# Attention followed by a mixture of experts: the last features turned by TensorE, the second expert prepared earlier, the loop count read later, output scatters without order

## Chip, cores and metric

One NeuronCore of a Trainium2 chip runs the whole program in one launch. The metric is device time in microseconds, median of the runs shown; lower is better.

## The reference

Eight batches of eight heads, 576 positions and 64 features go through causal attention with a decay from cumulated forget gates. The 4608 result rows (512 features) are then sent through one of eight experts each.

```python
decay = cum[:, :, :, None] - cum[:, :, None, :]
attn = softmax(where(causal, -1e9, scale * q @ k.T + decay))
x = (attn @ v).transpose(0, 2, 1, 3).reshape(4608, 512)
e_idx = argmax(x @ w_gate, axis=1)
gate_w = softmax(x @ w_gate)[e_idx];  eom = sigmoid(x @ w_output_gate)
for e in range(8):
    mask = e_idx == e
    out[mask] = gate_w * eom[mask, e] * (relu(x[mask] @ w1[e]) @ w2[e])   # 512 -> 1024 -> 512
```

## The kernel before

**Attention** (`attention`, lines 772 to 910) is a hand-written software pipeline: a loop over steps in which each part of the work has an offset in `OFF`, and the order of issue within a step is the string `OFF["order"]`. All engines run under a manual schedule, so each works through its instructions in the order of the program text. The features of a batch come in two units u = 0 to 15 (two per batch, four heads each). `feats` splits a unit into a high and a low f16 part (`x16`; ACT casts, DVE subtracts), `feats_turn` (line 527) turns each of the unit's four or five row tiles with a DMA transpose issued by SP into `xT`, and `feats_out` (line 534) writes `x16` to the DRAM buffer `xbuf`, also by SP. Units 0 to 14 are turned in the pipeline; unit 15 is made and turned behind it (lines 1039 to 1043).

**Routing** (`route`, lines 555 to 656) is a generator with one small operation per step: router matmuls on `xT`, argmax, rank within the expert, and at last one indirect DMA per row tile (POOL, line 649) that scatters row number and weight into the list `tbl`. Seven batches are routed in the pipeline; the last one is routed beside the first expert.

**Experts.** Rows of an expert are fetched by `gather_ids` (list from `tbl`, SP), `gather_rows` (indirect DMA by POOL, line 708) and `gather_turn` (DMA transpose by SP, line 714). Weights arrive as f32 (`fetch_w1`, `fetch_w2`, by SP, in four buffers each) and are split into f16 and bf16 parts by ACT and a subtraction (`split_w1`, line 666, `split_w2`, line 926). `up_products` and `up_split` make the hidden layer in eight column tiles fc (three matmuls for each of four k; ACT takes the high part out of PSUM, line 995, DVE the low one, line 996); `down_sum` makes one output tile of 128 rows (24 matmuls) and `down_out` (line 1017) evicts it by ACT and scatters it into the output by an indirect DMA of POOL.

**The start of the experts** (lines 1038 to 1080) is what the change is about. Expert 0 begins before the last batch is routed, on its first 384 rows, listed, gathered and turned in the pipeline (`early_gather`). Its order before: unit 15 is made and turned, first four W1 pieces of expert 1 fetched, the eight fc of expert 0 with steps of the last route between them (`OFF["steps"]`: one at fc 5, eight at 6, one at 7), three scatters of `tbl`, four W1 splits on DVE, the first output tile, `late_ids` (row numbers of the last 256 rows worked out on PE without waiting for `tbl`), gather and turn of these rows, the rest of the scatters, lists of expert 1, output tiles 1 and 2, gathers of expert 1, W1 pieces 4 to 7, the `up` of the late rows, turns of expert 1, two late output tiles, and at last all of W2 of expert 1 (line 1080).

**The main loop** (lines 1110 to 1146) runs expert 1 (n = 0) and then the other six, with the next expert's rows and weights fetched one stage ahead. In n = 0, behind the second output tile, `overflow_slots` (line 936) works out on DVE how many row tiles don't fit into the capacities, and reads that count into a register of every engine (line 972). The register is the bound of the loop of line 1148, behind everything.

Of the kernel before, what the change touches and what calls it, by code (L numbers as in the profile page):

```python
# [59 lines left out]
    "mv": ["xr", "v0", "v1"], "begin": -18, "wg": -4, "spread/1": -11,  # L60
    "before_late": 3, "steps": [0, 0, 0, 0, 0, 1, 8, 1], "dve": [181, 183, 185, 187, 189, 191],
    "order": "reduce put feats1 v0 scores nrec max pair rows spread feats0 fetch "
# [12 lines left out]
def _attn_moe(ctx, tc, qk, vm, f, wg, w1, w2, out):  # L75
# [451 lines left out]
    def feats_turn(u, t):  # L527
        b, hh = divmod(u, 2)
        if t < NC + b % 2:
            xT, x16 = xTs[u]  # L530
            nc.sync.dma_start_transpose(xT[:, t].rearrange("p j k n -> p (j k) n"),
                                        x16[:, t].rearrange("p j n -> p (j n)"))

    def feats_out(u):
        b, hh = divmod(u, 2)
        x16 = xTs[u][1]
        xv = xbuf[:, hh * DM:(hh + 1) * DM]
        nc.sync.dma_start(xv[b * S:b * S + SM].rearrange("(c p) d -> p c d", p=P),
                          x16[:, 0:NC].rearrange("p c j d -> p c (j d)"))
        if b % 2:  # L540
            for bb in (b - 1, b):
                r0 = (bb % 2) * SR
                nc.sync.dma_start(xv[bb * S + SM:(bb + 1) * S], x16[r0:r0 + SR, NC].rearrange("p j d -> p (j d)"))
# [228 lines left out]
    def attention():  # L772
# [12 lines left out]
        for s in range(OFF["begin"], last + OFF["nrest"] + 1):  # L785
# [36 lines left out]
            def turns():  # L822

                for t in range(NTB):
                    v, r = divmod(s - OFF["fturn"] - OFF["fturnstep"] * t, 12)
                    if r == 0 and 0 <= v < NQ - 1:
                        feats_turn(v, t)
# [108 lines left out]
    def overflow_slots():  # L936

        with tc.tile_pool(name="ov", bufs=1) as ov:
# [32 lines left out]
            nc.vector.tensor_copy(ncum, fl(cum)[0:1, E * G - 1:E * G])  # L971
        return nc.values_load(ncum, min_val=0, max_val=(NT - min(CAPS)) // P + E)

# [42 lines left out]

    def down_out(x, y, t):
        ids = x[0]
        ys = m2.tile([P, DM], F32, name="ys", bufs=3)
        nc.scalar.activation(out=ys, in_=y, func=AF.Copy, scale=ids[:, t, 1:2].bitcast(F32))  # L1020
        nc.gpsimd.indirect_dma_start(  # L1021
            out=out, out_offset=bass.IndirectOffsetOnAxis(ap=ids[:, t, 0:1], axis=0),
            in_=ys, in_offset=None, bounds_check=NT - 1, oob_is_err=False)

    def down(w2s, x, h, t0, t1):
        for t in range(t0, t1):
            down_out(x, down_sum(w2s, h, t), t)

# [3 lines left out]
    def load_w1(we, fc, raws=None, eng=nc.gpsimd):  # L1032
        return split_w1(m2, raws[fc] if raws else fetch_w1(m2, we, fc, 4), 8, eng)
# [3 lines left out]

    with tc.manual_schedule(engines=ENGINES):
        for part in range(2):
            feats(NQ - 1, part)  # L1040
            for t in (range(2), range(2, NTB))[part]:
                feats_turn(NQ - 1, t)
        feats_out(NQ - 1)
        late_before()
        W1r = [fetch_w1(m2, w1[1], fc, 4) for fc in range(4)]
        chain = route(B - 1)
        first = [(0, EARLY)]
        h = hidden()
        for fc in range(NF):
            hp = up_products(W1, x, first, fc)  # L1050
            for _ in range(OFF["steps"][fc]):
                next(chain, None)
            up_split(hp, h, first, fc)
        begun = len(scatters)
        while len(scatters) < begun + OFF["before_late"]:
            next(chain)
        W1n = [load_w1(w1[1], fc, W1r, nc.vector) for fc in range(4)]
        y = down_sum(W2, h, 0)
        at = late_ids()
        for t in range(ET, CT):  # L1060
            gather_rows(x, t, NT, at[:, t - ET:t - ET + 1])
            gather_turn(x, t)
        for _ in chain:
            pass
        down_out(x, y, 0)
        x1 = gather_ids(m2, tbl[NT:NT + CAP], CT)
        xl = gather_ids(m1, tbl[EARLY:CAP], CT - ET, ET, (m1.tile([P, CT, 2], I32, name="idsl"), x[1]))
        down(W2, x, h, 1, ET)
        for t in range(2):
            gather_rows(x1, t)  # L1070
        W1r += [fetch_w1(m2, w1[1], fc, 4) for fc in range(4, NF)]
        up(W1, x, [(EARLY, CAP)], h)
        for t in range(2, CT):
            gather_rows(x1, t)
        for t in range(CT):
            gather_turn(x1, t)
        W1n += [load_w1(w1[1], fc, W1r, nc.vector) for fc in range(4, NF)]
        down(W2, xl, h, ET, CT)
        W1, x = W1n, x1
        W2 = weights(load_w2, w2[1])  # L1080

# [28 lines left out]
        for n in range(len(CAPS) + 1):  # L1110
# [22 lines left out]
            for t in range(tiles):  # L1133
# [8 lines left out]
                down_out(x, y, t)  # L1142
                if not n and t == 1:
                    nsl = overflow_slots()
            if nx:
                e, x, W1, W2 = nx, x1, W1n, W2n

    with tc.For_i(0, nsl, 1) as i:
# [5 lines left out]
        h = up(weights(load_w1, w1[bass.ds(ei, 1)].rearrange("a f p k n -> (a f) p k n")), x, [(0, P)])  # L1154
        down(weights(load_w2, w2[bass.ds(ei, 1)].rearrange("a f p n -> (a f) p n")), x, h, 0, 1)

# [44 lines left out]
```

## Time and profile before

| | us |
|---|---|
| median of 3 runs (lowest to highest) | 821.77 (820.77 to 822.31) |
| the profiled execution, its own time | 827.2 |
| its span, first to last instruction | 825.5 |
| PE busy in it | 750.3 (91%) |
| POOL busy | 469.8 (57%) |
| DVE, ACT busy | 338.7, 338.6 (41% each) |

PE runs the matmuls; PEld is its weight load, which overlaps. An engine's time is busy time of instructions; a wait is told as the idle time before an instruction, with the event that came last. SP appears by its queue of DMA issues. The granted clock is TensorE's, as a share of 2.4 GHz.

### The profile page before, as it was taken

The page shows a single profiled execution, that of the slowest core. Times are in us where ns is not written, and L with a number is a line of the kernel's source. Part 1 is how long each engine was busy: PE and PEld are TensorE (multiplying, and loading weights), DVE is VectorE, ACT ScalarE, POOL GpSimd, SP SyncE. Part 2 cuts the span into 40 slices and gives each one's busy share as a digit, 9 for nine tenths or more (in the row PEclk, how much of TensorE's full clock was granted, in tenths as well). Part 3 has the DMA queues.
Part 4 walks back from the last instruction along what each step waited for, and adds up shares of the span by engine and source line. Part 5 has one row for each costly group of instructions (what it writes and reads, how often), then busy time and mean ns, then how long its engine had stood idle before and what let it go on. Part 6 is the DMA issues. An engine that isn't in the chain of part 4 may idle for free. (4 is left out here: it accounts for less than half of the span.)

```text
span 825.5 us, 21338 instructions
## 1 busy us (share of the span) xinstructions
PE 750.3 (91%) x8704; PEld 459.3 (56%) x8704; DVE 338.7 (41%) x774; ACT 338.6 (41%) x758; POOL 469.8 (57%) x517
## 2 busy tenths in 40 slices
PE   1699999899999999977979795999999999999995
PEld 0377777667776777755536462554544445444442
DVE  4446576575868576745502422120311203021020
ACT  6055565455655464644303321242342424333230
POOL 8088778688888888875143523345353644635321
PEclk9999999999999999989989897999999999999999
DMA  3343757958595678437868545265472745727210
GB/s 101 123 131 79 169 160 165 162 132 166 132 196 137 134 147 154 90 79 122 136 123 202 158 71 136 74 175 168 153 212 68 201 151 158 204 84 220 84 50 37
DMA packets 131689, 112.34 MB, mean 136 GB/s; under 512 B 94792, under 2 KB 104194, under 8 KB 131588
## 3 DMA queue, kind: packets, MB, share of 16 engines
q1 hardware_dynamic: 120020, 74.92, 40.4%
q10 hardware_dynamic: 4176, 17.11, 7.8%
q0 software_dynamic: 7392, 18.92, 7.7%
q8 instruction: 69, 1.13, 0.6%
q14 instruction: 32, 0.26, 0.1%
HBM read 72.52 MB, written 20.21 MB: 112 GB/s over the span
## 5 line engine op out<-in xcount | busy, mean ns | idle before, releaser
L380 POOL TENSOR_TENSOR plo<-p 128x512 f16<-128x512 f32 x186 | 197.5, 1076 | 69.5 <-ACT p L378 65.5
L986 PE MATMUL hp<-xT,w1h 128*128 128x512 f16 (+2 forms) x960 | 180.5, 304 | 16.2 <-DMA xT<-xg 9.9
L996 DVE SCALAR_TENSOR_TENSOR hl<-hp,hh 128x512 f16<-128x512 f32 (+2 forms) x120 | 54.0, 484 | 297.3 <-ACT hh L995 278.8
L296 DVE TENSOR_REDUCE nR<-mx 128x2 f32<-128x1024 f32 (+4 forms) x160 | 126.5, 807 | 92.2 <-PE mx L270 79.9
L378 ACT ACTIVATE p<-sc 128x512 f32<-128x512 f32 x192 | 112.8, 594 | 77.5 <-PE sc L270 69.1
L270 PE MATMUL sc<-qk 64*128 64x512 f32 (+4 forms) x640 | 136.7, 488 | 0.0
L1012 PE MATMUL y<-w2h,hh 128*128 128x512 f16 x312 | 119.2, 382 | 9.2 <-DVE ncum L971 9.2
L1013 PE MATMUL y<-w2l,hh 128*128 128x512 bf16 x312 | 119.2, 382 | 0.0
L1014 PE MATMUL y<-w2h,hl 128*128 128x512 f16 x312 | 119.0, 381 | 0.0
L986 PEld LDWEIGHTS <-w1h 128*128 128x128 f16 x960 | 76.3, 99 | 75.3 <-issue 13.4
L986 PE MATMUL hp<-xT,w1l 128*128 128x512 f16 (+2 forms) x480 | 114.3, 304 | 0.0
L995 ACT ACTIVATE hh<-hp 128x512 f16<-128x512 f32 (+2 forms) x120 | 46.8, 433 | 140.6 <-PE hp L986 132.7
L1021 POOL DMA_INDIRECT out_dram<-ys,ids x37 | 36.8, 995 | 102.5 <-ACT ys L1020 65.7
L270 PEld LDWEIGHTS <-pick 64*128 64x128 bf16 (+1 forms) x1152 | 64.1, 99 | 47.5 <-issue 25.6
L1020 ACT ACTIVATE ys<-y,ids 128x512 f32<-128x512 f32 x37 | 25.4, 687 | 137.2 <-issue 77.7
L930 POOL TENSOR_TENSOR w2l<-w2r,w2h 128x512 bf16<-128x512 f32 x28 | 32.2, 1153 | 82.1 <-ACT w2h L929 82.1
L270 PE MATMUL mx<-qk 64*128 64x256 bf16 (+5 forms) x384 | 64.6, 313 | 14.6 <-DVE nR L296 9.1
L452 PE MATMUL av<-Vs,p 128*128 128x65 f16 x640 | 69.9, 194 | 8.1 <-ACT xr L499 4.7
L454 PE MATMUL av<-Vs,plo 128*128 128x65 f16 x640 | 69.2, 193 | 4.6 <-POOL plo L380 4.6
L453 PE MATMUL av<-Vs,p 128*128 128x64 bf16 x640 | 69.5, 196 | 0.0
L270 PE MATMUL mx<-Ek,Eq 63*128 63x256 f16 (+5 forms) x384 | 58.5, 308 | 11.5 <-DMA Ek<-d 11.4
L670 POOL TENSOR_TENSOR w1l<-w1r,w1h 128x512 bf16<-128x512 f32 x48 | 54.6, 1162 | 21.5 <-ACT w1h L669 21.1
(178 smaller groups left out, 1380.7 us busy)
## 6 DMA issues: line engine op xcount, KB each, us to landing
qk<-in_qk_dram ACTq DMA_DIRECT2D x29, 576.0 KB
w1r<-in_w_dram SPq DMA_DIRECT2D x64, 256.0 KB
w2r<-in_w_dram SPq DMA_DIRECT2D x64, 256.0 KB
v<-in_vm_dram SPq DMA_DIRECT2D x16, 576.0 KB
xbuf<-x SPq DMA_DIRECT2D x16, 512.0 KB
qk<-in_qk_dram SPq DMA_DIRECT2D x3, 576.0 KB
xT<-x SPq DMA_TRANSPOSE x72
Eq<-mts SPq DMA_DIRECT2D x64, 0.1 KB
```

The costliest lines, as they stand in the source:

```text
L270: nc.tensor.matmul(dst(i), w(i), x(i), start=start, stop=stop)
L296: nc.vector.tensor_reduce(o, x, axis=AX.X, op=ALU.max, negate=True)
L378: nc.scalar.activation(out=f32, in_=src, func=AF.Exp, scale=0.125)
L380: eng.tensor_tensor(lo, f32, upper(f32), op=ALU.subtract)
L452: nc.tensor.matmul(dst, ph, vv[:, 0:W], start=kc == 0, stop=False)
L453: nc.tensor.matmul(dst[:, 0:D], ph, vv[:, W:].bitcast(BF16), start=False, stop=False)
L454: nc.tensor.matmul(dst, pl, vv[:, 0:W], start=False, stop=kc == qc)
L670: (eng or nc.vector).tensor_tensor(l, raw, h, op=ALU.subtract)
L986: nc.tensor.matmul(m[:, 0:c1 - c0], w[:, k], x, start=k == 0 and i == 0, stop=k == ND - 1 and i == 2)
L1012: nc.tensor.matmul(y, hh[:, fc, sl], wh, start=fc == 0, stop=False)
L1013: nc.tensor.matmul(y, hh[:, fc, sl], wl, start=False, stop=False)
L1014: nc.tensor.matmul(y, hl[:, fc, sl], wh, start=False, stop=fc == NF - 1)
```

## The change

The DMA transposes of units 14 and 15 go. `feats_turn_here` turns a unit with 20 transposes on TensorE into PSUM (tiles of the expert stage, two named hp1 and one y) and five evictions (three by ACT, two by DVE): unit 14 ahead of everything in the expert stage, unit 15 behind fc 1. The steps of the last route move forward, and so do the late rows (at fc 6, ahead of all five scatters of `tbl`). All eight W1 and W2 pieces of expert 1 are fetched and split in three portions of `ahead`, each in front of an output tile of expert 0, all subtractions on DVE; expert 1's gathers and turns all stand ahead of the late `up`. `overflow_slots` moves behind output tile 3 of n = 0 and its register read to output tile 0 of n = 2. Output scatters outside the loop are declared independent of one another.

```diff
-    "before_late": 3, "steps": [0, 0, 0, 0, 0, 1, 8, 1], ...
+    "steps": [0, 0, 1, 8, 1, 4, 4, 0], "turned": 1, "late": 6, ...
+    def feats_turn_here(u):
+        xT, x16 = xTs[u]
+        ms = [pm.tile([P, 512], F32, name=n, bufs=2).bitcast(F16) for n in ("hp1", "hp1", "y")]
+        for t in range(NTB):
+            for j in range(4):
+                nc.tensor.transpose(ms[t // 2][:, (t % 2 * 4 + j) * P:(t % 2 * 4 + j + 1) * P],
+                                    x16[:, t].rearrange("p j n -> p (j n)")[:, j * P:(j + 1) * P], identh)
+        for t in range(NTB):
+            dst, src = xT[:, t].rearrange("p j k n -> p (j k n)"), ms[t // 2][:, t % 2 * 512:t % 2 * 512 + 512]
+            if t % 2:
+                nc.vector.tensor_copy(dst, src)
+            else:
+                nc.scalar.copy(out=dst, in_=src)
...
-                    if r == 0 and 0 <= v < NQ - 1:
+                    if r == 0 and 0 <= v < NQ - 2:
                         feats_turn(v, t)
...
-        return nc.values_load(ncum, min_val=0, max_val=(NT - min(CAPS)) // P + E)
+        return ncum
...
+        if not looped:
+            for other in written:
+                tc.declare_no_dep(ins.ins, other.ins, reason="distinct rows")
+            written.append(ins)
...
+        feats_turn_here(NQ - 2)
         for part in range(2):
             feats(NQ - 1, part)
-            for t in (range(2), range(2, NTB))[part]:
-                feats_turn(NQ - 1, t)
         feats_out(NQ - 1)
         late_before()
         W1r = [fetch_w1(m2, w1[1], fc, 4) for fc in range(4)]
+        W2r = [fetch_w2(w2[1], fc) for fc in range(4)]
...
             for _ in range(OFF["steps"][fc]):
                 next(chain, None)
+            if fc == OFF["late"]:
+                at = late_ids()
+                for t in range(ET, CT):
+                    gather_rows(x, t, NT, at[:, t - ET:t - ET + 1])
+                    gather_turn(x, t)
             up_split(hp, h, first, fc)
-        begun = len(scatters)
-        while len(scatters) < begun + OFF["before_late"]:
-            next(chain)
-        W1n = [load_w1(w1[1], fc, W1r, nc.vector) for fc in range(4)]
-        y = down_sum(W2, h, 0)
-        at = late_ids()
-        for t in range(ET, CT):
-            gather_rows(x, t, NT, at[:, t - ET:t - ET + 1])
-            gather_turn(x, t)
+            if fc == OFF["turned"]:
+                feats_turn_here(NQ - 1)
+        W1n, W2n = [], []
+        def ahead(fc):
+            W1n.append(load_w1(w1[1], fc, W1r, nc.vector))
+            if fc + 4 < NF:
+                W1r.append(fetch_w1(m2, w1[1], fc + 4, 4))
+            W2n.append(split_w2(W2r[fc], nc.vector))
+            if fc + 4 < NF:
+                W2r.append(fetch_w2(w2[1], fc + 4))
         for _ in chain:
             pass
-        down_out(x, y, 0)
+        for fc in range(3):
+            ahead(fc)
+        down_out(x, down_sum(W2, h, 0), 0)
         x1 = gather_ids(m2, tbl[NT:NT + CAP], CT)
         xl = gather_ids(m1, tbl[EARLY:CAP], CT - ET, ET, ...)
-        down(W2, x, h, 1, ET)
-        for t in range(2):
+        for fc in range(3, 6):
+            ahead(fc)
+        down_out(x, down_sum(W2, h, 1), 1)
+        for t in range(CT):
             gather_rows(x1, t)
-        W1r += [fetch_w1(m2, w1[1], fc, 4) for fc in range(4, NF)]
-        up(W1, x, [(EARLY, CAP)], h)
-        for t in range(2, CT):
-            gather_rows(x1, t)
+        for fc in range(6, NF):
+            ahead(fc)
+        down_out(x, down_sum(W2, h, 2), 2)
         for t in range(CT):
             gather_turn(x1, t)
-        W1n += [load_w1(w1[1], fc, W1r, nc.vector) for fc in range(4, NF)]
+        up(W1, x, [(EARLY, CAP)], h)
         down(W2, xl, h, ET, CT)
-        W1, x = W1n, x1
-        W2 = weights(load_w2, w2[1])
+        W1, W2, x = W1n, W2n, x1
...
-                if not n and t == 1:
-                    nsl = overflow_slots()
+                if n == 0 and t == 3:
+                    ncum = overflow_slots()
+                if n == 2 and t == 0:
+                    nsl = nc.values_load(ncum, min_val=0, max_val=(NT - min(CAPS)) // P + E)
```

## Rows read from the trace of the kernel before

**Rows 1.** Busy time by stretch (the view of windows): stretch from : to in us, its length, busy us and instruction count of PE, PEld, DVE, ACT and POOL, then the granted TensorE clock (1.00 is 2.4 GHz), the DMA share and GB/s. The first four are stretches right behind an idle time of PE, the last is the kernel's second half.

```profile
388.30:391.80 3.50, 3.49 (x12) 1.68 (x13) 0.00 (x0) 0.00 (x0) 2.28 (x3) 0.51 0.63 140
...
428.40:432.70 4.30, 4.30 (x21) 3.05 (x22) 0.42 (x1) 0.38 (x1) 0.87 (x1) 0.50 0.90 282
...
464.50:470.40 5.90, 5.86 (x23) 3.30 (x23) 1.11 (x3) 0.00 (x0) 2.07 (x2) 0.51 0.60 181
...
506.60:511.30 4.70, 4.66 (x12) 1.64 (x12) 0.00 (x0) 1.14 (x2) 2.26 (x2) 0.50 0.62 40
...
525.00:817.20 292.20, 292.20 (x1750) 141.86 (x1748) 53.55 (x112) 98.59 (x205) 126.53 (x121) 1.00 0.49 142
```

**Rows 2.** What PE waited for from 384 us to the end (the view of waits): the waiting instruction <- its releaser: total us, times, longest us.

```profile
PE hp L986 <- DMA xT<-xg: 9.9, 2, 5.7
PE y L1012 <- DVE ncum L971: 9.2, 1, 9.2
PE hp L986 <- DVE hl L996: 5.6, 1, 5.6
PE hp L986 <- issue: 0.7, 1, 0.7
```

**Rows 3.** The timeline of PE between 384 and 425 us: start, us, engine, line, operation, out<-in, count, and in brackets the idle time before it and what ended it.

```profile
383.88 0.18 PE L609 MATMUL rk<-runs,ones 128*128 128x32 bf16 x1
388.31 0.76 PE L986 MATMUL hp<-xT,w1h 128*128 128x384 f16 x2 [4.26 <-DMA xT<-xg]
...
422.31 0.38 PE L1014 MATMUL y<-w2h,hl 128*128 128x512 f16 x1
```

**Rows 4.** The timeline of SP's DMA queue from 380 to 450 us (issue times).

```profile
380.74 1.19 SPq L531 DMA_TRANSPOSE xT<-x  x1
382.02 2.63 SPq L714 DMA_TRANSPOSE xT<-xg  x2
...
392.42 8.67 SPq L531 DMA_TRANSPOSE xT<-x  x5
...
404.26 0.46 SPq L731 DMA_DIRECT2D had<-tbl  x1
404.76 1.92 SPq L663 DMA_DIRECT2D w1r<-in_w_dram  x4
423.56 2.68 SPq L714 DMA_TRANSPOSE xT<-xg  x2
426.51 0.39 SPq L702 DMA_DIRECT2D ids<-tbl  x1
```

**Rows 5.** The timeline of POOL from 356 to 384 us.

```profile
360.50 1.25 POOL L649 DMA_INDIRECT tbl<-rec,pi  x1 [0.17 <-issue]
...
371.77 1.34 POOL L708 DMA_INDIRECT xg<-xbuf,ids  x1 [0.15 <-issue]
```

**Rows 6.** The timeline of SP's DMA queue from 363 to 384 us.

```profile
366.00 0.40 SPq L702 DMA_DIRECT2D ids<-tbl  x1
...
375.57 1.23 SPq L714 DMA_TRANSPOSE xT<-xg  x1
```

**Rows 7.** The timeline of POOL from 408 to 424 us.

```profile
410.48 1.48 POOL L649 DMA_INDIRECT tbl<-rec,pi  x1 [1.79 <-DVE so L634]
...
414.05 0.96 POOL L649 DMA_INDIRECT tbl<-rec,pi  x1 [0.22 <-issue]
415.32 1.06 POOL L708 DMA_INDIRECT xg<-xbuf,lids  x1 [0.30 <-issue]
```

**Rows 8.** The timeline of PE from 424 to 530 us: two of the 128x256 matmul groups at full clock.

```profile
433.45 0.38 PE L986 MATMUL hp<-xT,w1h 128*128 128x256 f16 x2
433.67 0.27 PE L986 MATMUL hp<-xT,w1l 128*128 128x256 f16 x1
433.77 0.38 PE L986 MATMUL hp<-xT,w1h 128*128 128x256 f16 x2
```

**Rows 9.** The instructions of line 345 (the kernel's only transposes on TensorE), with duration min/median/max in ns.

```profile
L345 PE MATMUL mt<-identh,mh x32: 222/222/272, 26.5 to 357.4; 128*9 128x128 f16 x32
```

**Rows 10.** The timeline of ACT from 378 to 530 us: one eviction of each kind, with the idle time before it.

```profile
396.04 0.49 ACT L995 ACTIVATE hh<-hp 128x384 f16<-128x384 f32 x1 [1.46 <-PE hp L986]
...
422.73 0.69 ACT L1020 ACTIVATE ys<-y,ids 128x512 f32<-128x512 f32 x1 [4.49 <-PE y L1014]
...
435.94 0.38 ACT L995 ACTIVATE hh<-hp 128x256 f16<-128x256 f32 x1 [0.93 <-PE hp L986]
```

**Rows 11.** The timeline of DVE from 378 to 530 us.

```profile
387.19 0.42 DVE L147 TENSOR_TENSOR x<-xr,x 128x256 f16<-128x256 f32 x1
...
505.95 0.13 DVE L971 CAST ncum<-ov 1x1 int32<-1x1 f32 x1
```

**Rows 12.** Groups of ACT's instructions by line between 400 and 470 us: count, busy us, mean ns, idle before.

```profile
L669 ACT CAST w1h<-w1r 128x512 f16<-128x512 f32 x8 | 4.5, 619 | 0.3 <-DMA w1r<-in_w_dram 0.3
```

**Rows 13.** The same for DVE.

```profile
L670 DVE TENSOR_TENSOR w1l<-w1r,w1h 128x512 bf16<-128x512 f32 x8 | 5.0, 685 | 0.0
```

**Rows 14.** The instructions of line 972 (the loop count's read), duration min/median/max in ns.

```profile
L972 PEldq TENSOR_LOAD <-ncum x1: 487/487/487, 506.1 to 506.1; - x1
```

**Rows 15.** The timeline of POOL from 812 us to the end.

```profile
813.11 0.97 POOL L1021 DMA_INDIRECT out_dram<-ys,ids  x1 [4.21 <-ACT ys L1020]
819.76 0.98 POOL L1021 DMA_INDIRECT out_dram<-ys,ids  x1 [5.69 <-POOLq L1148]
```

More of the change, by code (lines that the diff above doesn't have):

```diff
@@ L60 @@
     "mv": ["xr", "v0", "v1"], "begin": -18, "wg": -4, "spread/1": -11,
-    "before_late": 3, "steps": [0, 0, 0, 0, 0, 1, 8, 1], "dve": [181, 183, 185, 187, 189, 191],
+    "steps": [0, 0, 1, 8, 1, 4, 4, 0], "turned": 1, "late": 6, "dve": [181, 183, 185, 187, 189, 191],
     "order": "reduce put feats1 v0 scores nrec max pair rows spread feats0 fetch "
@@ L1015, in down_sum, with down_out @@
         return y
-    def down_out(x, y, t):
+    written = []
+    def down_out(x, y, t, looped=False):
         ids = x[0]
@@ L1020, in down_out, with down @@
         nc.scalar.activation(out=ys, in_=y, func=AF.Copy, scale=ids[:, t, 1:2].bitcast(F32))
-        nc.gpsimd.indirect_dma_start(
+        ins = nc.gpsimd.indirect_dma_start(
             out=out, out_offset=bass.IndirectOffsetOnAxis(ap=ids[:, t, 0:1], axis=0),
             in_=ys, in_offset=None, bounds_check=NT - 1, oob_is_err=False)
-    def down(w2s, x, h, t0, t1):
+        if not looped:
+            for other in written:
+                tc.declare_no_dep(ins.ins, other.ins, reason="distinct rows")
+            written.append(ins)
+    def down(w2s, x, h, t0, t1, looped=False):
         for t in range(t0, t1):
-            down_out(x, down_sum(w2s, h, t), t)
+            down_out(x, down_sum(w2s, h, t), t, looped)
     def weights(load, we):
@@ L1154, in _attn_moe @@
         h = up(weights(load_w1, w1[bass.ds(ei, 1)].rearrange("a f p k n -> (a f) p k n")), x, [(0, P)])
-        down(weights(load_w2, w2[bass.ds(ei, 1)].rearrange("a f p n -> (a f) p n")), x, h, 0, 1)
+        down(weights(load_w2, w2[bass.ds(ei, 1)].rearrange("a f p n -> (a f) p n")), x, h, 0, 1, True)
 _INS = ['q', 'k', 'v', 'f', 'moe_w_gate', 'moe_w_output_gate', 'moe_w1', 'moe_w2']
```

## The prediction

> **What bounds the kernel now.** I read the page's slices of PE first: behind the start, those below 8 tenths all lie between 350 and 520 us. The view by stretch says it sharply: from 525 to 817 us PE works 292.20 of 292.20 us at full clock [rows 1], so nothing there can be won without taking matmuls away, which the change doesn't do. What can be won is PE's idle time in the start of the experts. The list of PE's waits behind 384 us has 9.9 us in two waits for turned rows, 9.2 for the loop count, 5.6 for DVE and 0.7 without a releaser [rows 2], 25.4 in all. The reader should then look at what follows each long wait: four stretches of 3.5, 4.3, 5.9 and 4.7 us at a granted clock of 0.50 or 0.51 [rows 1], the lower level of 1.2 GHz. The engine had stood still for 4.26, 5.7, 5.6 and 9.2 us before them; the 0.7 us one is followed by no such stretch. Half of these 18.4 us, 9.2, is lost too. So at most 25.4 + 9.2 = 34.6 us lie there.
>
> **The change part by part.** Each PE wait is taken in order, in the profiled execution's time.
>
> *First wait (turned rows of expert 0, 4.26 us).* PE ends attention at 383.88 + 0.18 = 384.06 and starts the up at 388.31 [rows 3]. SP issued the second and third early turns from 382.02 to 384.65, behind a unit 14 turn that started only at 380.74 [rows 4]; landing took 388.31 - 384.65 = 3.66. The first early turn started at 375.57 [rows 6], 2.46 behind the end of its gather (371.77 + 1.34) [rows 5]. Without the unit 14 turn the other two can be issued some 3.7 earlier, at 380.9, and land near 384.6. PE meanwhile does the 20 transposes of unit 14. No row shows such a block transpose in sequence. From below: three 128x256 matmuls follow one another in 433.77 - 433.45 = 0.32 [rows 8], 0.055 per 128 columns; from above: the one existing transpose lasts 0.222 alone [rows 9]. Back to back in independent PSUM columns they are nearest to the former: 20 x 0.055 = 1.1. The up starts at 385.2 instead of 388.31 (-3.1), and without a long idle time the half clock goes too (-1.75): -4.85.
>
> *Unit 15 on TensorE:* another 1.1 us on the path, +1.1. Its source was ready at 387.19 + 0.42 [rows 11]; unit 14's three ACT evictions of 0.6 (the mean of a 128x512 ACT cast is 0.619 [rows 12]) push it to about 389.2, and two fc of 1.95 each (eviction 0.49 and 1.46 idle before it [rows 10]) end on PE at 385.2 + 3.9 = 389.1. The cover is exact, so I add nothing but keep 1 us for the range. Ten SP turns of 1.2 to 1.7 us (five in 8.67) [rows 4] go; nothing on PE waited for them, but SP comes to its weight fetches at about 395 instead of 404.76 [rows 4]. There the read of the row list stands in front (it was at 404.26 [rows 4]) and must now wait for the scatters of batch 6; that wait is inside the 395.
>
> *Second wait (late rows, 5.66 us; half clock 2.15; and the 0.7).* Before, the late gathers started at 415.32, behind three scatters of the list [rows 7], and their turns at 423.56 [rows 4]. Now the row numbers are ready after fc 6, near 402.5, the two gathers end near 405, and with the 2.46 of rows 5 and 6 they land near 407.5, the turns near 412.5. PE ends the three early output tiles (5.18 each: 0.69 and 4.49 idle [rows 10]) at about 419.5, against 422.31 + 0.38 = 422.69 before [rows 3], so the late up finds its rows. All three go: -8.5.
>
> What is late next is the weights' last portion. The five scatters stand behind the gathers on POOL, cost 1.3 to 1.8 each with what lies between (410.48 to 414.05 held two, 414.05 to 415.32 one) [rows 7], and end near 412.5. Expert 1's list was read 366.00 - (360.50 + 1.25) = 4.25 behind the last scatter [rows 5, 6], so near 416.7 SP goes on, and only then fetches W1 and W2 piece 7, which stand behind this read on SP. Two 256 KB pieces land 2.5 to 4 us later. ACT does two casts of 0.62 [rows 12] on them, then the third output tile, and only then the first late hidden tile, which is due at 420.8; with two PSUM buffers PE runs on until 422.2. DVE's subtraction of 0.685 [rows 13] stands in the same way. With the fastest landing PE waits 0.9 us, with the slowest that I find without a further fault 3. I take 2.0: +2.0.
>
> *Third wait (DVE, 5.59 us, half clock 2.95).* It comes from the W2 splits of expert 1 standing ahead of its first hidden tiles on ACT and DVE; they are now done at 423. Expert 1's rows need lists, five gathers and five turns, about 435, while PE arrives near 442. -8.5.
>
> *Fourth wait (loop count, 9.20 us, half clock 2.35).* PE stood until the count was cast at 505.95 [rows 11]. Behind tile 3 of n = 0 the same DVE chain ends beside the first hidden tile of n = 1, and at n = 2 the count is long there. What stays is the read itself, 0.487 on PE [rows 14]: at least 0 if matmuls already issued cover it, at most its length. -11.55 + 0.5 = -11.05.
>
> *Output scatters* never gate PE. At the end the last scatter starts 819.76 - 813.11 = 6.65 behind the one before it [rows 15], 1.47 more than the tile time of 5.18. Without the wait for its predecessor that may shrink; between -1.5 and +0.5 I take 0, since the last eviction still has to come first.
>
> Sum: -4.85 + 1.1 - 8.5 + 2.0 - 8.5 - 11.05 = -29.8 us. The span would be 825.5 - 29.8 = 795.7. The profiled execution took 827.2, 5.4 over the median of 821.77; I take the difference over to the median: **792.0 us**.
>
> **Rivals.** *A. The late rows come later and the front stays short of weights.* For it: the one late gather in the trace ended at 415.32 + 1.06 = 416.38 and its turn started 7.2 us later [rows 4, 7], not 2.46. Then SP holds all six following fetches back, the last pieces land near 423.5, and PE waits 3.4 us and gets the half clock again (2.15): 3.6 more than the 2.0 taken. Also for it: the scatter at 410.48 took 1.48 us and the one at 414.05, when DVE was idle, 0.96 [rows 7]; sixteen DVE subtractions now stand beside the five scatters, 5 x 0.5 = 2.5. 792.0 + 3.6 + 2.5 = 798.1 us. Against: the slow gather had three scatters before it.
>
> *B. Transposes are dear.* If each holds PE for its 0.222 [rows 9], 40 cost 8.9 instead of 2.2: 798.7 us. The Trainium skill (VectorE: DVE Perf Modes, The three transpose paths) gives 390 ns for a 128x128 transpose on TensorE; by it the sum would lose 13.4 us and the time would be 805.4. No row here shows that figure, and the 0.222 is already a lone instruction with its latency.
>
> *C. The loop count only moves its wait.* If the chain at the new place were late for n = 2, the 11.05 come back: 803.0 us. Against: two whole experts lie between.
>
> *D. Slower.* SP stands at the read of expert 1's list, in front of weight pieces 7, and with it ACT, the late up and all of PE. It would have to stand there 30 us longer than I say to eat the gain; from then on the time passes 822, say 826. Against: the longest wait behind a list in these rows is 4.25.
>
> **How the numbers follow.** The forecast's own bounds are 787 (no weight wait, no read, tail 1.5 shorter, transposes a little under 0.055) and 796 (3 us of weight wait, 1 of cover, dearer transposes). Chances: forecast 0.71, A 0.14, B 0.07, C 0.04, D 0.04. The range 786 to 801 holds the forecast, A and the nearer price of B. All but D are faster by more than 0.2%, about what a measurement of this kernel can tell from no change; same 0.01 comes off D: faster 0.96, same 0.01, slower 0.03.
>
> **What would show it.** PE's waits behind 384 us fall from 25 us to under 5, and no stretch at 0.5 clock is left there. The transposes stand 0.055 apart, between attention and the first up. Late turns start before 410 and weight piece 7 is the last release of the late up. No idle time in n = 0; a bubble of up to 0.5 at n = 2. I am wrong if a wait over 4 us is left, which brings its half clock along, or if the transposes stand 0.2 apart.

## The result: 22 us faster, 8 us short of the forecast

| | before | changed | ratio (95%) |
|---|---|---|---|
| median of 4 runs, us | 822.04 (820.77 to 823.83) | 799.96 (798.0 to 801.74) | 0.9729 (0.970 to 0.9759) |
| profiled execution, us (span) | 827.2 (825.5) | 798.0 (796.3) | |
| mean granted clock | 0.971 | 0.987 | |
| attention ends at, us | 384.06 | 378.55 | |
| from there to the end, us | 441.44 | 417.75 | |

The forecast was 792.0 us, 786 to 801. The two profiles differ by 29.2 us, but 5.5 of these lie in the attention, from which the change takes only the DMA turns of unit 14. Its end moved between 378.5 and 389.6 us over the profiles of this study (x1 and x4 left aside), and with the same attention on one chip between 383.8 and 389.5 (x0, x5, x6, x7), so these 5.5 us can't be put down to the change. So I compare the stage behind it: span less the end of attention's last matmul (line 609 before [rows 3], 624 after). It fell by 23.7 us, where 29.8 had been forecast. Two of the experiments' profiles, x1 and x4, were taken in a disturbed execution; of these I read what waits for what, and the sizes only roughly.

What PE waited for from 378 us to the end (waiting instruction <- releaser: total us, times, longest us); it answers to [rows 2]. Helpers moved: the up is line 1001 now, its eviction 1010 and 1011.

```profile
PE hp L1001 <- DVE hl L1011: 5.6, 1, 5.6
PE hp L1001 <- DMA xT<-xg: 1.1, 1, 1.1
```

Of 25.4 us of waits 6.7 are left. The wait for the loop count is gone, and so are the late rows' and expert 1's row waits. The timeline of PE at the two places:

```profile
378.37 0.18 PE L624 MATMUL rk<-runs,ones 128*128 128x32 bf16 x1
378.40 1.05 PE L540 MATMUL hp<-identh,x 128*128 128x128 f16 x16
379.29 0.39 PE L540 MATMUL y<-identh,x 128*128 128x128 f16 x4
380.82 0.48 PE L1001 MATMUL hp<-xT,w1h 128*128 128x384 f16 x2 [1.15 <-DMA xT<-xg]
...
416.99 0.27 PE L1001 MATMUL hp<-xT,w1l 128*128 128x256 f16 x1
422.83 0.58 PE L1001 MATMUL hp<-xT,w1h 128*128 128x256 f16 x2 [5.57 <-DVE hl L1011]
```

Sixteen transposes take (379.29 - 378.40) / 16 = 0.056 us each. The second wait stands in the late rows' up: PE fills both PSUM buffers, then stops until the first late hidden tile is out. By stretch (from : to, length, busy us of PE, PEld, DVE, ACT and POOL, granted clock, DMA share, GB/s), as in [rows 1]:

```profile
422.83:427.40 4.57, 4.57 (x22) 3.18 (x22) 0.70 (x2) 0.38 (x1) 3.35 (x5) 0.50 0.82 213
...
525.00:787.00 262.00, 262.00 (x1541) 125.38 (x1539) 44.08 (x92) 87.34 (x178) 114.91 (x110) 1.00 0.49 143
```

Of the four half-clock stretches one is left, behind the 5.57 us wait; it costs 4.57 / 2 = 2.3 us more. Cut into sections by PE's first matmul of each kind:

| section | before | changed | difference | forecast |
|---|---|---|---|---|
| attention's end to first output tile | 22.68 | 20.39 | -2.3 | -3.75 |
| three early output tiles | 15.95 | 15.54 | -0.4 | 0 |
| late rows: gap and up | 19.2 | 18.5 | **-0.7** | **-6.5** |
| late rows' tiles and expert 1's up | 45.0 | 36.5 | -8.55 | -8.5 |
| expert 1's down | 37.5 | 25.9 | -11.6 | -11.05 |
| the rest | 292.8 | 292.6 | -0.2 | 0 |

The last row ends with PE's last matmul; 8.3 and 8.2 us follow it. One row is far off. What held the first late hidden tile is seen on ACT, which evicts it at line 1010 (casts of the second expert's pieces at 684 and 944, output tiles at 1037):

```profile
405.46 0.62 ACT L944 CAST w2h<-w2r 128x512 f16<-128x512 f32 x1
415.15 0.62 ACT L684 CAST w1h<-w1r 128x512 f16<-128x512 f32 x1 [9.07 <-DMA w1r<-in_w_dram]
416.53 0.62 ACT L944 CAST w2h<-w2r 128x512 f16<-128x512 f32 x1 [0.76 <-DMA w2r<-in_w_dram]
...
420.19 0.62 ACT L684 CAST w1h<-w1r 128x512 f16<-128x512 f32 x1 [0.18 <-DMA w1r<-in_w_dram]
...
421.36 0.68 ACT L1037 ACTIVATE ys<-y,ids 128x512 f32<-128x512 f32 x1
421.94 0.65 ACT L1010 ACTIVATE hh<-hp 128x256 f16<-128x256 f32 x2
```

ACT stood 9.07 us for piece **4** of W1, then had four pairs of casts and two output tiles to do before line 1010. For piece 7, which the forecast had named, it stood 0.18. SP's queue tells when the pieces were asked for (issue times):

```profile
394.19 0.38 SPq L746 DMA_DIRECT2D had<-tbl  x1
394.62 1.88 SPq L678 DMA_DIRECT2D w1r<-in_w_dram  x4
396.55 1.85 SPq L938 DMA_DIRECT2D w2r<-in_w_dram  x4
404.34 2.62 SPq L729 DMA_TRANSPOSE xT<-xg  x2
407.06 1.65 SPq L678 DMA_DIRECT2D w1r<-in_w_dram  x1
...
416.02 0.42 SPq L678 DMA_DIRECT2D w1r<-in_w_dram  x1
```

Piece 4 was issued at 407.06, behind the late rows' turns, and cast 8.1 us later. The queue's own waits from 378 to 420 us say what held it: the read of the list (line 746) stood 8.7 us for batch 6's scatters, the late turns 5.9 us for their rows.

```profile
SPq L746 <- DMA tbl<-rec,pi: 8.7, 1, 8.7
...
SPq L729 <- DMA xg<-xbuf,lids: 5.9, 1, 5.9
```

### The profile page after: what moved, and what is told of

Read it like the earlier page. It is cut to its first block, busy times and chain, and to the rows that moved or that the text cites. A ratio compares the mean times of both kernels' runs of the same rounds, so it can differ in the third digit from the quotient of the medians.

```text
span 796.3 us, 21422 instructions
## 1 busy us (share of the span) xinstructions
PE 741.1 (93%) x8744; PEld 457.0 (57%) x8744; DVE 342.1 (43%) x782; ACT 342.5 (43%) x764; POOL 465.8 (58%) x513
## 5 line engine op out<-in xcount | busy, mean ns | idle before, releaser
L1001 PE MATMUL hp<-xT,w1h 128*128 128x512 f16 (+2 forms) x960 | 177.2, 300 | 6.7 <-DVE hl L1011 5.6
L270 PE MATMUL sc<-qk 64*128 64x512 f32 (+4 forms) x640 | 134.9, 482 | 0.0
L1037 ACT ACTIVATE ys<-y,ids 128x512 f32<-128x512 f32 x37 | 25.4, 687 | 124.3 <-issue 67.7
L945 POOL TENSOR_TENSOR w2l<-w2r,w2h 128x512 bf16<-128x512 f32 x24 | 27.6, 1150 | 77.7 <-ACT w2h L944 77.7
L453 PEld LDWEIGHTS <-p 128*128 128x128 bf16 x640 | 59.9, 98 | 6.4 <-issue 6.3
```

What stands on the lines that cost most here:

```text
L270: nc.tensor.matmul(dst(i), w(i), x(i), start=start, stop=stop)
L453: nc.tensor.matmul(dst[:, 0:D], ph, vv[:, W:].bitcast(BF16), start=False, stop=False)
L1001: nc.tensor.matmul(m[:, 0:c1 - c0], w[:, k], x, start=k == 0 and i == 0, stop=k == ND - 1 and i == 2)
```

## The experiments

Open after the traces: which parts carry the gain, whether the slow pieces are a matter of transfers (and what slows them) or of the order on an engine, and whether the missing 6 us can be had. Each kernel is the changed one with one edit, unless it says otherwise. "Stage" is the time from attention's end to the end, read from one profile of each.

| run | us | before, same chip | ratio (95%) | stage | PE's wait for late hidden tiles |
|---|---|---|---|---|---|
| x0 changed, again | 808.42 | 834.31 | 0.9711 (0.9665 to 0.9756) | 419.6 | 5.4 |
| x1 late turns behind pieces | 804.69 | 829.21 | 0.9685 (0.9634 to 0.9736) | 421.5 | 0 |
| x2 count read early | 815.69 | 829.21 | 0.9828 (0.9779 to 0.9877) | 431.0 | 7.0 |
| x3 scatters ordered | 804.52 | 829.21 | 0.9691 (0.9632 to 0.9749) | 418.6 | 5.2 |
| x4 features turned by DMA | 820.77 | 829.21 | 0.9868 (0.9808 to 0.9927) | 431.8 | 10.0 |
| x5 without last lists | 812.47 | 834.31 | 0.9735 (0.9686 to 0.9783) | 423.7 | 4.7 |
| x6 weights ahead of list | 815.75 | 834.31 | 0.9804 (0.9753 to 0.9855) | 426.6 | 13.3 |
| x7 seven buffers | 810.90 | 834.31 | 0.9697 (0.9619 to 0.9774) | 421.5 | 2.8 |
| x8 no lists, weights ahead | 813.05 | 833.68 | 0.9766 (0.9693 to 0.9838) | 423.3 | 4.0 |
| a1 before, count later | 820.89 | 833.68 | 0.9876 (0.9822 to 0.9931) | 430.5 | (7.3 in two) |
| x9 casts behind late tiles | 803.39 | 833.68 | 0.9652 (0.9608 to 0.9696) | 421.6 | 0.6 |
| x10 the same again | **793.45** | 822.07 | **0.9668 (0.9624 to 0.9712)** | **410.5** | 0 |

The stages of x5 and x8 can't be set beside the others as they stand. What follows PE's last matmul takes 14.98 us in both, 8.1 to 8.5 in all other runs, nearly all of it without work on any engine; why isn't shown. The changed kernel's stretch and then x5's (columns as above):

```profile
788.11:796.30 8.19, 0.00 (x0) 0.00 (x0) 0.00 (x0) 0.69 (x1) 0.98 (x1) 0.78 0.07 23
...
796.80:811.78 14.98, 0.00 (x1) 0.00 (x0) 0.00 (x0) 0.69 (x1) 0.97 (x1) 0.67 0.02 6
```

From attention's end to PE's last matmul the stage is 408.7 us in x5 and 408.3 in x8, against 411.3 in x0 and 409.6 in the changed kernel's first profile. Their ratios carry the same 6.8 us, 0.8%.

**x0**, the changed kernel on another chip, gives the base for the others.

> The changed kernel itself, for comparison on the same chip: ratio 0.973 to the kernel before; from the end of attention to the end 417 to 419 us; PE waits 5 to 6 us in the late up for DVE.

The chip was slower for both kernels; stage and wait came out alike (419.6 and 5.4, against 417.75 and 5.6).

### What carries the gain

**x2** puts the read of the count back behind tile 1:

```
-                if n == 0 and t == 3:
+                if n == 0 and t == 1:
                     ncum = overflow_slots()
-                if n == 2 and t == 0:
                     nsl = nc.values_load(ncum, ...)
```

> The changed kernel with the loop count worked out and read behind output tile 1 of n = 0, as before. Theory (the term of 11.05 us of the prediction is right): PE waits 9 us there and runs 4.7 us at half clock, 811 us. Rival (the count's wait was covered by something else that is late there anyway): under 4 us more, 803 us.

The stage is 12.4 us above x3 on the same chip, and the section in which the wait falls, expert 1's down, takes 38.0 us instead of 25.9. In the waits of PE (380 us to the end) the count stands there again, with its size of [rows 2]:

```profile
PE y L1027 <- DVE ncum L986: 9.2, 1, 9.2
PE hp L1001 <- DVE hl L1011: 7.0, 1, 7.0
```

**a1** is the converse: the kernel before with this part alone.

```
-        return nc.values_load(ncum, ...)
+        return ncum
...
-                if not n and t == 1:
-                    nsl = overflow_slots()
+                if n == 0 and t == 3:
+                    ncum = overflow_slots()
+                if n == 2 and t == 0:
+                    nsl = nc.values_load(ncum, ...)
```

> The kernel before with one part of the change alone: the loop count is read behind the first tile of the expert after next, no longer right behind the slots. My step (the wait of 11.55 us for the count goes, a read of 0.5 us stays): the stage behind attention falls from 441.4 by 11 us to 430 to 431, the ratio to the kernel before is 0.986 to 0.988, and the wait for the count is gone from TensorE. Rival C (the wait only moves to the later read, or another takes its place): the stage falls by under 4 us, the ratio is above 0.995.

The stage fell by 11.0, from 441.44 to 430.5 (another chip), the ratio is 0.9876. Expert 1's down takes 25.9 us, as in the changed kernel, instead of 37.5. Both directions agree: 11 to 12 us of the gain are this part, and nothing of its size takes its place.

**x4** gives both last features back to the DMA's turns:

```
-                    if r == 0 and 0 <= v < NQ - 2:
+                    if r == 0 and 0 <= v < NQ - 1:
                         feats_turn(v, t)
...
-        feats_turn_here(NQ - 2)
         for part in range(2):
             feats(NQ - 1, part)
+            for t in (range(2), range(2, NTB))[part]:
+                feats_turn(NQ - 1, t)
...
-            if fc == OFF["turned"]:
-                feats_turn_here(NQ - 1)
```

> The changed kernel with units 14 and 15 turned by DMA as before, everything else as changed. Theory (the turns of unit 14 delay the early rows, those of unit 15 keep SP and the DMA engines busy for 9 us, and the route's first step at fc 2 now needs them early): PE waits 4 us at the start, and again 6 to 9 us at the router matmuls, each with its half clock, 812 us. Rival (the weights' wait of 5.6 us absorbs most of it): 803 us.

PE's waits show that the turns are missed in three places: the late hidden tiles (5.6 before this edit), the router's product, which reads the last features, and the early rows (1.1).

```profile
PE hp L1001 <- DVE hl L1011: 10.0, 1, 10.0
PE lg L578 <- DMA xT<-x: 5.0, 1, 5.0
PE hp L1001 <- DMA xT<-xg: 4.6, 1, 4.6
```

The ratio rose from 0.9711 to 0.9868: the transposes are worth some 1.6% (13 us), more than the 3.75 that I had written beside them. I take it that the later steps on SP and POOL hang behind them, which the waits suggest and no run shows by itself. It is the gain of the part within the changed order, not alone.

**x3** lets each output scatter wait for the one before it again (`if not looped:` becomes `if False:`).

> The changed kernel with the output scatters ordered one behind the other, as before. Theory (scatters gate nothing): 800 us, within 1 us of the changed kernel. Rival (they hold POOL in front of the gathers of expert 1, so rows come late, or lengthen the tail): 2 us or more, 802 us and above.

No difference: 418.6 beside x0's 419.6, and ratios of 0.9691 and 0.9711 whose intervals overlap. In the changed kernel the last scatter still waits on its own queue, at POOL's tail, where [rows 15] had 5.69:

```profile
790.63 0.98 POOL L1038 DMA_INDIRECT out_dram<-ys,ids  x1 [5.68 <-POOLq L1182]
```

### Why the late hidden tiles wait

**x1** issues the pieces 4 to 6 ahead of the late turns on SP.

```
             if fc == OFF["late"]:
                 ...
                     gather_rows(x, t, NT, at[:, t - ET:t - ET + 1])
-                    gather_turn(x, t)
...
         for fc in range(3):
             ahead(fc)
+        for t in range(ET, CT):
+            gather_turn(x, t)
```

> The changed kernel with one thing moved: the two DMA turns of the late rows are issued by SP behind the first portion's six weight fetches instead of in front of them. Theory 1 (SP stands at the late turns until their gather has landed, and with it the fetch of W1 piece 4, on which ACT waits 9.07 us): the fetch is issued near 401 us instead of 407.06, ACT's wait for it falls under 2 us, PE's 5.57 us wait in the late up and the half clock behind it (2.2 us) go, 792 us. Theory 2 (the DMA engines are full: 2 MB of first pieces, gathers and turns): the fetch is issued earlier but lands as late, the wait stays over 4 us, 799 us. Theory 3 (the wait moves to the late turns, which now stand behind 1.5 MB of weights): a PE wait for turned rows of 2 to 5 us, 796 us.

The wait for hidden tiles is gone, and one of 9.6 us for the late rows' turns stands in its place. The ratio, 0.9685 beside 0.9691 of x3 on the same chip, shows neither gain nor loss. SP spent 12.48 us on the two turns:

```profile
421.19 12.48 SPq L729 DMA_TRANSPOSE xT<-xg  x2
```

**x5** takes the last batch's five list scatters out of the work (`if b == B - 1: continue` ahead of the scatter), to see whether they slow the transfers beside them.

> The changed kernel without the five list scatters of the last batch (left out of the work: its rows enter no expert's list but the late rows). Theory 4 (behind a group of list scatters of 8 bytes a row the DMA engines are busy at a tenth of their throughput until the scatters have landed, and the turns and weight pieces 4 to 6 lie in that time): the transfers behind 403 us run at 200 GB/s or more, piece 4 lands within 4 us of its issue, PE's 5.6 us wait and its half clock go, 410 us behind attention. Theory 1 (SP's order alone) : piece 4 is still issued at 407 behind the turns and PE still waits 3 us or more, 415 us.

They do, for the late turns above all. I aligned the two runs at the first packet of the late turns (405.5 us in the changed kernel, 417.3 in x5). In the first two microseconds they move 178 and 186 GB/s, nearly the same. The view of DMA over the next four, with the line of queue q1 (packets, MB, share of 16 engines), the changed kernel (407.5 to 411.5 us) first:

```profile
DMA packets 653, 0.17 MB, mean 41 GB/s; under 512 B 653, under 2 KB 653, under 8 KB 653
q1 hardware_dynamic: 651, 0.17, 130.9%
```

x5 (419.3 to 423.3 us):

```profile
DMA packets 1075, 1.11 MB, mean 277 GB/s; under 512 B 673, under 2 KB 673, under 8 KB 1075
q1 hardware_dynamic: 995, 0.84, 77.1%
```

and the first of x5's four microseconds alone (419.3 to 420.3):

```profile
DMA packets 640, 0.18 MB, mean 184 GB/s; under 512 B 624, under 2 KB 624, under 8 KB 640
```

The last third of the turns, some 650 packets under 512 B, takes all four microseconds with the scatters. Without them 624 of its packets move in the first one, at 184 GB/s, and the weight pieces follow in larger packets, at 370 GB/s from 421 to 425 us. So the like comparison is 41 against 184; the 277 hold weight pieces too. The queue is no less occupied in the slow case. The Trainium skill (DMA: Bandwidth & Descriptors, Specifications) asks for 512 B and more per transfer for the full rate. The turns' 178 and 186 beside the pieces' 370 agree with it, though a turn is another kind of transfer too; the 41 are this case's own. Piece 4 in x5 was issued at 418.89 and cast at 422.31, 3.4 us later instead of 8.1:

```profile
422.31 0.62 ACT L686 CAST w1h<-w1r 128x512 f16<-128x512 f32 x1 [3.04 <-DMA w1r<-in_w_dram]
```

Yet PE's wait only fell to 4.7 us, from 5.4 in x0 on the same chip, where the list read came as late behind attention's end (18.6 us, x5 18.4). Piece 4 is cast 34.2 us behind that end instead of 38.9, and the first late hidden tile is out at 42.1 instead of 44.9; but the late up begins 2.2 us earlier too, at 35.4 instead of 37.6. So the wait hardly moves, while the stage to PE's last matmul is 2.6 us shorter. The slow stretch is real but not the whole cause: from piece 4's cast at 422.31 ACT still has 7.8 us of casts and output tiles in front of the hidden tile (6.8 in the changed kernel).

**x6** sets the first eight fetches ahead of that list read (`late_before()` moved behind the two lists of fetches).

> The changed kernel with the first eight weight fetches issued by SP in front of the list read had (which waits 8.7 us for the scatters of batch 6) instead of behind it. Theory 1 and 4 (the front is a queue on SP and in the DMA engines; what is issued 9 us earlier is out of the way when the late rows and pieces 4 to 6 come): late turns start 2 us earlier, ACT's wait for piece 4 falls from 9 to 4 us or less, PE's wait from 5.6 to 1 or less, 411 us behind attention. Rival (the early pieces are slowed by batch 6's scatters instead, and had comes so late that the late row numbers hold DVE): PE waits 3 us or more at the first output tile, no gain, 418 us.

Worse: the wait is 13.3 us. The second four fetches took SP 9.57 us, and for 8.1 of them it stood for writes of the features into `xbuf`:

```profile
394.05 9.57 SPq L938 DMA_DIRECT2D w2r<-in_w_dram  x4
403.80 0.38 SPq L746 DMA_DIRECT2D had<-tbl  x1
```

and of SP's waits:

```profile
SPq L717 <- DMA tbl<-rec,pi: 12.7, 1, 12.7
...
SPq L938 <- DMA xbuf<-x: 8.1, 3, 6.0
```

Beside x0 on the same chip, the list read came 1.0 us later, and the late turns and pieces 4 to 6 were issued no later (28.3 and 31.0 us behind attention's end, 28.4 and 31.2 in x0). What came later is what hangs on that read by way of POOL: the late gathers by 3.5 us, the last list scatter by 4.8. The read of expert 1's list (line 717) then stood 12.7 us for the scatters, and piece 7 behind it was issued at 47.7 us instead of 38.9. ACT waited for piece 4 as before, and again for piece 7, the one that the forecast had named:

```profile
421.29 0.62 ACT L684 CAST w1h<-w1r 128x512 f16<-128x512 f32 x1 [9.62 <-DMA w1r<-in_w_dram]
...
434.69 0.62 ACT L684 CAST w1h<-w1r 128x512 f16<-128x512 f32 x1 [2.80 <-DMA w1r<-in_w_dram]
```

**x7** gives the raw pieces seven buffers instead of four, and fetches seven pairs at the front.

> The changed kernel with seven raw buffers for W1 and W2 in place of four, and pieces 0 to 6 fetched at the front, so that nothing but piece 7 waits behind the late turns on SP. Theory 1 (SP's order): pieces 4 to 6 land by 409 us, PE's 5.6 us wait is gone, 411 us behind attention. Theory 4 (the engines stand behind the list scatters): 3.5 MB of weights run into that time, pieces 5 and 6 land behind 412 us and the late turns, now behind them in the queue, behind 416: PE waits 2 to 5 us for turned rows instead, 415 us.

The wait for hidden tiles is 2.8, but 2.5 us for an output tile's buffer, 2.4 for turned rows and 1.4 without a releaser have come. The late turns took 10.70 us to issue behind 14 pieces. Again the wait moved. The ratio, 0.9697 beside x0's 0.9711 on the same chip, is the same within the intervals.

**x8** joins x5 and x6.

> Two holds taken away at once: the five list scatters of the last batch are left out of the work (the lists then lack that batch), and the first eight fetches of the second expert's weights stand ahead of the read of the list on SyncE. Theory 4 with both holds (the read that waits for the scatters of the batch before, and the slow stretch behind the last batch's scatters): the second half of the pieces, fetched behind the late turns, lands within 3 to 4.5 us of its issue as in the run without scatters alone, and TensorE's wait for the late rows' hidden values falls from 4.7 us there to under 2; the stage is 417 to 420. Rival 6 (the front is short of transfer time with or without the scatters): the wait stays at 4 us or more and the stage at 423 or above.

Neither side is borne out whole. The wait is 4.0, rival 6's number, while the stage of 423.3 is above 423 only by the long tail; with a tail like the others' it would be 416.5, below what theory 4 expected. Piece 4 was issued at 421.29 and cast at 424.23, so the pieces do land fast, but the list read was issued 19.8 us behind attention's end, and ACT had 7.3 us of casts and output tiles from 424.23 to the first late hidden tile at 431.50. Making the pieces land sooner is worth some 1 to 3 us of stage here, with needed work left out, and doesn't take PE's wait away.

**x9** leaves all transfers in place and changes an order on ACT and DVE: the casts and subtractions of pieces 4 to 7 go between the late rows' hidden tiles instead of ahead of them.

```
-        for fc in range(3, 6):
-            ahead(fc)
+        ahead(3)
         down_out(x, down_sum(W2, h, 1), 1)
...
-        for fc in range(6, NF):
-            ahead(fc)
         down_out(x, down_sum(W2, h, 2), 2)
...
-        up(W1, x, [(EARLY, CAP)], h)
+        lcols = [(EARLY, CAP)]
+        for fc in range(NF):
+            up_split(up_products(W1, x, lcols, fc), h, lcols, fc)
+            if fc % 2:
+                ahead(4 + fc // 2)
```

> The changed kernel with one order different on ScalarE and VectorE: the casts and subtractions of the second expert's pieces 4 to 7 come between the evictions of the late rows' up products (one pair after every second block of them), no longer ahead of them. Fetches, turns and scatters keep their places on their queues. Theory 5 (the wait of 5.6 us for the late rows' hidden values is an order on ScalarE: their eviction stands behind four pairs of casts that wait for pieces fetched into the slow stretch behind the list's scatters, and nothing needs these pieces yet): TensorE's wait for the late rows' hidden values falls below 1 us, the half clock behind it goes, the stage behind attention gets 5.5 to 8 us shorter than the changed kernel's 417.8 (410 to 412), the ratio to the kernel before falls to 0.963 to 0.967. Rival 6 (the pieces themselves are the limit, wherever the casts stand): the wait comes back inside the late rows' products or ahead of the next expert's fifth block, and the stage stays at 415 to 419. Rival 7 (the late rows' turns land in the same slow stretch and are next): a wait for the turned rows of 3 us or more takes its place.

The wait of 5.6 fell to 0.6 and is not the late rows' (it stands at 403.81, in the early rows' up), but PE waited 3.8 and 1.7 us for expert 1's turned rows, so the stage was no shorter, against the 410 to 412 expected; the ratio, 0.9652, is as expected. The profiled execution took 810.44 us, the other five 801.40 to 806.43. Was the row wait the next link, or this execution? **x10** runs the same kernel again, on the next chip.

> The same kernel as in the run with the casts behind the late rows, on whatever chip comes next. There TensorE's wait for the late rows' hidden values was gone (0 of 5.6 us), and waits of 3.8 and 1.7 us for the second expert's turned rows stood in its place, in a profile whose read of the expert's list took 8.0 us to land against 5.4 in the profile of the changed kernel. If that landing is what the transfers of one execution happen to give, the wait for the second expert's rows is 0 to 3 us here and the stage behind attention 411 to 417; if the rows are simply next in the chain whatever the execution (rival 7), the wait is 4 to 7 us again and the stage 419 to 423. The ratio to the kernel before is 0.961 to 0.970 in either case.

That chip gave the kernel before 822.07 us, as for the first result. The whole of PE's waits from 376 us on:

```profile
PE hp L1001 <- DMA xT<-xg: 1.4, 2, 1.2
PE av L452 <- ACT xr L499: 0.2, 1, 0.2
```

The stage is 410.5, 7.2 us below the changed kernel's first profile. The ratios say less: 0.9668 and 0.9652 (x9) beside the changed kernel's 0.9729 and 0.9711 and x3's 0.9691, a gain of 0.2 to 0.8%, some 2 to 6 us. x9's interval lies below that of the changed kernel's first result, x10's overlaps it by a little (0.9712 against 0.970), and both overlap x0's. So that the wait goes is shown twice; how much time that gives is less sure.

In x9 the read of expert 1's list was issued 38.6 us behind attention's end and its rows' gathers began at 46.6; in x10 they stand at 35.0 and 41.5. The last list scatter was issued at 30.6 and 27.6. So x9's row wait came with lists and rows that were 3 to 5 us later in that execution, and there the rows are indeed next in the chain. ACT in x10 has the late hidden tiles first, the casts in its idle time:

```profile
415.68 0.69 ACT L1037 ACTIVATE ys<-y,ids 128x512 f32<-128x512 f32 x1 [4.49 <-PE y L1029]
416.98 0.38 ACT L1010 ACTIVATE hh<-hp 128x256 f16<-128x256 f32 x1 [0.62 <-PE hp L1001]
...
418.57 0.61 ACT L684 CAST w1h<-w1r 128x512 f16<-128x512 f32 x1
419.08 0.62 ACT L944 CAST w2h<-w2r 128x512 f16<-128x512 f32 x1
```

and the clock stays up through the late rows' up:

```profile
420.00:425.00 5.00, 4.98 (x47) 4.30 (x45) 3.69 (x8) 3.08 (x7) 3.15 (x3) 1.00 0.39 114
```

Its late rows' up takes 10.7 us, the 18.5 of the changed kernel less the 5.57 wait and the 2.3 of half clock. The edit moves DVE's subtractions along with ACT's casts, and no run takes the two apart. In the changed kernel's trace DVE had the last of its own subtractions in front of the late hidden tile, and then stood for ACT's:

```profile
421.49 0.69 DVE L945 TENSOR_TENSOR w2l<-w2r,w2h 128x512 bf16<-128x512 f32 x1
422.35 0.76 DVE L1011 SCALAR_TENSOR_TENSOR hl<-hp,hh 128x256 f16<-128x256 f32 x2 [0.17 <-ACT hh L1010]
```

So the two were 0.17 us apart, and by this trace moving the work of one alone would have left the other's in front of the tile.

## Why the forecast was near, and which term was off

799.96 lies in the range of 786 to 801, but above the forecast's own bounds of 787 to 796: the upper end was there for the rivals. The prediction's own sign of being wrong, a wait of over 4 us with its half clock behind it, is in the trace. So most parts were sized well, one was not, and that the whole stayed in the range owes something to its width.

1. **What bounds the kernel** was read rightly. All of the stage's gain lies in PE's idle time and half-clock stretches between attention and expert 2, and the second half stayed as it was (292.8 and 292.6).
2. **First wait and the transposes**: -2.3 instead of -3.75. The transposes cost what I took (0.056 each, forecast 0.055), so rival B falls. The 390 ns that the Trainium skill (VectorE: DVE Perf Modes, The three transpose paths) gives for one transpose is not what one costs in a row of them here. Of the 3.7 us by which the early turns were to come earlier, 1.6 came: without the feature turns between, the three turns took SP 7.01 us in all (370.52 to 377.53, that is 1.02 ahead of attention's end, against 0.59 behind it), so 1.15 us of wait is left. No half clock follows it.
3. **Second wait and the weights: the step that failed.** I wrote -8.5 and +2.0; it was -0.7 together. The late rows were in time, as the step says. The term "+2.0" named the right engine and the right order (casts, third tile, hidden tile), but the wrong piece and size. I timed it from piece 7 behind the list read, with the one landing in my rows (4.25 behind a scatter). The wait came from piece 4, fetched behind the late turns among the list's scatters, 8.1 us to its cast, with all other casts behind it: 5.57 us of idle time and, what I had left out, 2.3 us of half clock behind it. 7.9 instead of 2.0 is nearly all of the 6.1 us by which the stage missed. x5 shows the slow transfers, x9 and x10 that the order on ACT and DVE turned them into PE's wait. Rival A had the half clock and a wait of 3.4 and came to 798.1, near the measured 799.96; it blamed SP's six fetches, which is the right queue, and the late rows, which it isn't. Its reading of one late gather misses a second one in that trace, which its sum doesn't use. Its closeness is partly luck: 2.5 of its us were for list scatters slowed by DVE, of which three of the five took 1.31 to 1.50 us and two 0.97, and PE waited for none of them.
4. **Third and fourth wait**: -8.55 and -11.6 against -8.5 and -11.05. The register read shows no idle time at all, so its 0.5 was too much; x2 and a1 confirm the size of the fourth. Rival C falls.
5. **Scatters and tail**: 0, as written (x3). Rival D falls: behind the list read SP stood 2.9 us.
6. The step from span to median: of the 5.4 us by which the profile stood over its runs, I could not know that 5.5 lay in the attention; the changed profile stands 2 us below its median, and the difference in attention can't be told from its spread.

## What to carry to other kernels

When prefetched work is put ahead on a queue in program order, ask of every engine what stands behind its first wait: here four pairs of casts that nobody needed yet, with their subtractions, held the one eviction that PE was waiting for, and moving them behind it took the wait away in both runs, where three other orders of the transfers (x1, x6, x7) gave nothing that can be told from noise, or a loss. A wait's price includes the half clock behind it: each wait of 3.8 us and more behind the attention was followed by it in these profiles, so a term that leaves such a wait should carry that from the start. And compare stages, not spans, when a part that the change doesn't touch moves by several us from run to run.

## What the runs showed of the hardware

- The lists' scatters (8-byte rows) slow what runs beside them: the late turns' last third moved at 41 GB/s with them and at 184 without. The last batch's landed 8.0 to 11.1 us after their issue in the changed kernel, those of all batches 4.1 to 11.1 with a median of 6.6. The forecast's 4.25 counts from the end of the last scatter's issue to the list read; so counted, the two reads of the changed kernel came 9.3 (line 746) and 7.3 us (line 717) behind.
- 20 transposes on TensorE in sequence took 1.1 us, at 0.056 each, and the granted clock stayed at 1.00 (378.55 to 398.94 us, one wait of 1.15 in it).
- A turn by DMA held SP's queue for 1.3 us in quiet stretches (2.62 for two), but 10.70 for two behind 14 weight pieces, with scatters beside them (x7).
- Half clock does not follow the length of a wait alone. In x7 PE ran at half clock behind a wait of 2.48 us, and at full clock behind one of 2.82 (at 423.09 and 445.05):

```profile
423.30:426.70 3.40, 3.18 (x9) 1.19 (x9) 1.97 (x5) 1.97 (x5) 1.00 (x1) 0.50 0.97 64
...
445.00:449.00 4.00, 3.89 (x30) 2.95 (x31) 1.18 (x4) 0.77 (x2) 0.00 (x0) 1.00 1.36 178
```
